# Sums of weight quarters, made once and fetched, in the second layer of an attention and two-FFN kernel

## The chip, the core and the metric
The kernel runs on one core of one Trainium2 chip. The metric is the device time of one execution in microseconds (us); a comparison uses the median of several runs. The profile is one further execution taken by the hardware profiler. The engines are named as the profile names them: PE (TensorE, matmuls; PEld its weight loads), DVE (VectorE), ACT (ScalarE), POOL (GpSimd) and SP (SyncE, which only issues transfers here).

## What is computed
Three stages follow each other, all in float32.
```
attention: 4 batches x 8 heads, 576 x 64; scores below (row maximum - tau) are masked,
           softmax, times v                                  -> x1, 2304 tokens x 512
layer 1:   sigmoid(x1 @ w_gate) * (x1 @ w_val) @ w_out       -> x2   (hidden 1536)
layer 2:   h = x2 @ w_in;  g = h if h >= 1, 0 if h <= -1, else (h + 1)^2 / 4
           g @ w_out                                         -> out  (hidden 2048)
```

## The kernel before
**Tokens and weights.** After attention the 2304 tokens are worked on in 3 passes of T = 768. Each matmul on float32 data is three: each operand is split into a rounded part that ScalarE copies and a remainder that VectorE subtracts (high by high, high by low, low by high). Activations stay in SBUF (`xall`); weights are converted once during attention and layer 1 by a chain of VectorE operations (`conversions`), written to DRAM (`saved`), and loaded again for each pass. `conversions` is a generator: a step of layer 1 takes a fixed number of items from it (`ops`), each about one VectorE operation, so that they lie beside the matmuls. Layer 1 is 36 steps (3 passes by 12 blocks of the hidden dimension): up matmuls (L480 to L482), sigmoid and product, then the down matmuls of the step before (L730).

**Layer 2** is 24 pairs of hidden blocks, 8 in each pass; pairs are numbered 0 to 23 here, so passes meet at pairs 7/8 and 15/16. The up matmul of a pair is done block-wise with seven products in place of eight, on sums of quarters. On the token side these are `x_sums`: four POOL operations a pass (L558 to L561, on 128x768), whose results and the plain quarters are split by `x_split` (L567 on ScalarE, L568 on VectorE) into seven blocks, numbered x0 to x6 and used by products 0 to 6. On the weight side they are `w_sums`: four POOL subtractions of 128x256 a pair (L576) into one tile `tsum`; `w_split` (L582, L583) splits the plain quarters and `tsum` (128x1024).

**A pair** (`pair`) issues seven products of six matmuls (L607) into two PSUM banks. Product 0's result is drained by ScalarE into `s1` (L676, the first drain); product 1's is added to it by VectorE (L665, the pair's first sum); product 3 needs the bank of that sum again. Product 2 lands on top of product 0 and is drained as `u2` (L688, the second drain); products 3 to 6 end in four more VectorE sums, of which the first is `u3` and frees the bank for product 5, and the last belongs to product 6. Then follow the activation's parts for the pair's two halves: two ScalarE squares (L615, L616), a two-input VectorE operation (L618, "STT"), the rounded half `hh` (L619) and the remainder `hl` (L621). The down matmuls (`down_pair`, 36 of them, L712) of a pair run on PE after the up matmuls of the next pair, so PE alternates: up of pair q, down of pair q - 1. `out_split` (L592, L593) splits the pair's two down weights.

**The order.** Each engine runs its own instructions in the order in which they are written. Work that lies beside matmuls is put in a list by `due(at, release, last, cost, what)` and taken out by `fill(slot, room)`: slot 3q stands behind the first drain of pair q, 3q + 1 behind its first sum, and 3q + 2 behind its last sum, that is beside the down matmuls. `fill` issues whatever has been released, by `at`, as long as `room` holds the cost, and at slot `last` in any case. All loads and stores are issued by SP, also in order: an SP instruction that waits holds the ones behind it. `finish` drains layer 1's last result (in pair 1), `store` an output pass (in pairs 9 and 17, and at the end).

Of the kernel before, what the change touches and what calls it, by code (L numbers as in the profile page):

```python
# [29 lines left out]
def kernel(  # L30
# [68 lines left out]
    }  # L99
    wides = [ps_w.tile([P, 2, 512], F32, name=f"w{i}") for i in range(3)]  # L100
# [353 lines left out]
    def ffn(att):  # L454


        with ExitStack() as st:
# [4 lines left out]
            xsp, hts = {}, {}  # L462

# [20 lines left out]
            def conversions():  # L484


                for j, (ph, f, gs) in enumerate(todo):
                    if j == 0:
                        extract(ph, gs, highs[0])
                    dst = turn() if ph == 0 else w2s[j % 2]  # L490
                    if ph == 0:
                        w32[0, 0, f] = dst
                    ops = convert(ph, gs, highs[j % 2], dst)
                    for m, _ in enumerate(ops):
                        if m == 3 + len(gs):
                            for g in todo[j + 2][2] if j + 2 < len(todo) else ():
                                load_w(todo[j + 2][0], g)
                        if m < 4 + len(gs):
                            yield
                    nc.sync.dma_start(out=saved[ph, f], in_=dst[:, : len(gs) * KD * P])  # L500
                    if j + 1 < len(todo):
                        extract(*todo[j + 1][::2], highs[(j + 1) % 2])
                    yield

# [35 lines left out]
            NQ = NF[1] // 2  # L540
            HK = KD // 2
            HC = HK * P
# [27 lines left out]
            def w_sums(q):  # L570

                w0, w1 = (w32[q][i] for i in range(2))
                b11, b21, b12, b22 = (w[:, i * HC : (i + 1) * HC] for w in (w0, w1) for i in range(2))
                t2, t3, t1, t4 = (tsum[:, i * HC : (i + 1) * HC] for i in range(4))
                for o, a, b in ((t1, b12, b11), (t2, b22, t1), (t3, b22, b12), (t4, b21, t2)):
                    nc.gpsimd.tensor_tensor(o, a, b, op=ALU.subtract)  # L576

# [11 lines left out]
            def out_split(q, i):  # L589
                src = w32[q][i][:, KD * P : 2 * KD * P]  # L590
                oh, ol = wout(q, i)
                nc.scalar.activation(oh, src, AF.Copy)  # L592
                nc.vector.tensor_tensor(ol, src, f32(oh), op=ALU.subtract)  # L593

# [50 lines left out]
            def due_x(t):  # L645
                q = t * NQ
                for i in range(7):
                    first = 3 * (q - 1) + min(i, 2)
                    last = 3 * q - 1 if i == 0 else 3 * q if i == 1 else 3 * q + 1
                    due(start(q) + i - 1, first, last, 0.93, lambda i=i: x_split(t, i))  # L650
# [7 lines left out]
            def pair(q):  # L658
# [14 lines left out]
                for i in range(2):  # L673
                    due(at - 1, 3 * q, 3 * q + 2, 0.67, lambda i=i: out_split(q, i))
                product(0, ps)
                nc.scalar.activation(s1, ps[0], AF.Copy)  # L676
                fill(3 * q, 1.9)
# [3 lines left out]
                if more:  # L681
                    w_sums(q + 1)
# [15 lines left out]
                for i in range(2):  # L698
                    g = activate(i, c[i], h[i])
                    for early, cost in ((4, 0), (3, 0.92), (1.5, 0.92)):  # L700
                        last = 3 * q + 3 if i == 0 else 3 * q + 5
                        due(at + 4 * i - early, 3 * q + 2, last, cost, lambda g=g: next(g))
                fill(3 * q + 2, LEN(q) - 7.7)
# [31 lines left out]
            def finish(t, y, slot=None):  # L735

                for i, (a, b, d) in enumerate(spans):
                    dst = xall[:, d, t * T + a - d * T : t * T + b - d * T]
                    if i % 2 == 0:
                        w = lambda dst=dst, a=a, b=b: nc.vector.tensor_copy(dst, at(y, a, b))  # L740
                    else:
                        w = lambda dst=dst, a=a, b=b: nc.scalar.activation(dst, at(y, a, b), AF.Copy)
                    if slot is None:
                        w()
                    else:
                        due(start(slot // 3) + 0.1 * i, slot, slot + 1, (1 - i % 2) * (b - a) / 800, w)

            def store(t, y, i, slot=None):
# [7 lines left out]
                def work():  # L756
                    for a in range(2) if end else (slice(None),):
                        if (i + a if end else i) % 2 == 0:
                            nc.vector.tensor_copy(o[:, a], src[:, a])
                        else:  # L760
                            nc.scalar.activation(o[:, a], src[:, a], AF.Copy)
                        nc.sync.dma_start(out=dst[:, a], in_=o[:, a])

                if slot is None:
                    work()
                else:
                    due(start(slot // 3) + 0.1 * i, slot, slot + 1, (1 - i % 2) * 0.67, work)
# [62 lines left out]
            for s in range(NS):  # L830
                nxt = order[s + 1] if s + 1 < NS else None
                ops = 8 if order[s][1] == 0 else 5
# [13 lines left out]
                elif s == NS - 2:  # L846
                    load_pair(0)
                    w_sums(0)
# [5 lines left out]
                if s == NS - 1:  # L854
# [4 lines left out]
                    fill(-1, 2.7)  # L859
# [7 lines left out]
            for q in range(NPASS * NQ):  # L867
                pair(q)
                if q == 0:
                    down(*order[-1][1:], y)  # L870
                    finish(NPASS - 1, y, 3)
                elif q < NPASS * NQ - 1:
# [3 lines left out]
                    if q % NQ == 0:  # L876
                        for i in range(T // P):
                            store(q // NQ - 1, y, i, 3 * q + 3)
# [56 lines left out]
```

## Time and profile before
| | |
|---|---|
| three runs | 1189.24, 1191.58, 1191.53 us; median 1191.53 |
| the profiled execution | 1189.46 us |
| its span, first to last instruction | 1187.6 us |
| PE, DVE, ACT, POOL busy | 95%, 72%, 52%, 23% of the span |
| mean granted clock of PE | 0.986 of full |

Matmuls are pipelined and their ends are modelled, so start times say more than busy shares. In a row of the timeline the time in brackets is how long the engine was idle before it and what ended the wait. L numbers are lines of the kernel before.

### The profile page before, as it was taken

The numbers are of one execution on the slowest core, as the hardware profiler recorded it, in microseconds if no ns is written. First come the engines' busy times: TensorE is split into PE (matmuls) and PEld (weight loads), VectorE is DVE, ScalarE is ACT, GpSimd is POOL, SyncE is SP. The second block draws the span as 40 slices with busy tenths as digits, with TensorE's granted clock in tenths as the row PEclk, the third lists the DMA queues.
The fourth block names the chain that finished last, engine by engine and source line by source line (L and its number), as shares of the span: only waits on it lengthen the run. The fifth ranks groups of instructions, "written<-read, shape, count | busy, mean of one in ns | idle before, by whom it ended". The sixth has DMA issues, their size and how long they took to land. (4 is left out here: it accounts for less than half of the span.)

```text
span 1187.6 us, 17358 instructions
## 1 busy us (share of the span) xinstructions
PE 1124.1 (95%) x6372; PEld 950.4 (80%) x6372; DVE 859.2 (72%) x1440; ACT 617.4 (52%) x1048; POOL 270.9 (23%) x423
## 2 busy tenths in 40 slices
PE   8999999999799999999999999799898998899998
PEld 5555565566799999999999999788787887778886
DVE  7888888885899988665685643676776766776663
ACT  5777777776444434433443323555455554655552
POOL 3444454453000000000000030222531234312310
PEclk9999999999899999999999999999998998999999
DMA  4323322313564665435534331122211212123101
GB/s 126 95 84 78 91 73 57 80 49 121 175 207 160 215 211 186 170 107 177 185 103 164 116 124 54 36 71 72 71 36 63 100 69 71 36 89 107 36 1 53
DMA packets 59380, 122.30 MB, mean 103 GB/s; under 512 B 8976, under 2 KB 35232, under 8 KB 59296
## 3 DMA queue, kind: packets, MB, share of 16 engines
q1 hardware_dynamic: 59152, 121.20, 31.2%
q8 instruction: 50, 0.82, 0.3%
q14 instruction: 34, 0.28, 0.1%
q10 hardware_dynamic: 144, 0.00, 0.0%
HBM read 98.57 MB, written 22.62 MB: 102 GB/s over the span
## 5 line engine op out<-in xcount | busy, mean ns | idle before, releaser
L480 PE MATMUL pgv<-xflat,win 128*128 128x384 f32 x560 | 188.5, 337 | 6.9 <-ACT act L520 4.1
L481 PE MATMUL pgv<-xflat,win 128*128 128x384 f32 x560 | 188.2, 336 | 0.0
L482 PE MATMUL pgv<-xflat,win 128*128 128x384 f32 x560 | 188.2, 336 | 0.0
L712 PE MATMUL w<-wout,hh 128*128 128x512 f32 x576 | 184.3, 394 | 0.6 <-ACT hh L619 0.6
L730 PE MATMUL w<-hh,wout 128*128 128x512 f32 (+1 forms) x576 | 147.3, 338 | 0.0
L607 PE MATMUL pu<-xflat,win 128*128 128x384 f32 x576 | 117.5, 362 | 29.2 <-DVE vals L665 28.8
L607 PEld LDWEIGHTS pu<-xflat,win 128*128 128x128 f32 x576 | 108.4, 204 | 38.2 <-DVE vals L665 33.4
L259 DVE TENSOR_SCALAR_CACHE_REDUCE s<-w,nscale 128x576 f32<-128x576 f32 x144 | 112.7, 816 | 32.8 <-PE w L250 23.0
L712 PEld LDWEIGHTS w<-wout,hh 128*128 128x128 f32 x576 | 108.1, 188 | 25.4 <-ACT hh L619 1.0
L524 DVE TENSOR_TENSOR act<-pgv,act 128x384 f32<-128x384 f32 x70 | 38.8, 554 | 118.7 <-PE pgv L482 115.1
L712 PE MATMUL w<-wout,hl 128*128 128x512 f32 x288 | 113.7, 395 | 0.5 <-DVE hl L621 0.5
L480 PEld LDWEIGHTS pgv<-xflat,win 128*128 128x128 f32 x560 | 105.7, 189 | 9.5 <-ACT act L520 4.7
L279 DVE SCALAR_TENSOR_TENSOR p<-s,mx,ex 128x576 f32<-128x576 f32 x144 | 111.9, 810 | 0.5 <-POOL lt L286 0.5
L271 ACT ACTIVATE ex<-s,mx 128x576 f32<-128x576 f32 x144 | 104.8, 775 | 6.2 <-DVE s L259 5.8
L730 PEld LDWEIGHTS w<-hh,wout 128*128 128x128 f32 x576 | 98.7, 189 | 11.4
L481 PEld LDWEIGHTS pgv<-xflat,win 128*128 128x128 f32 x560 | 105.8, 189 | 1.7 <-DVE xflat L472 0.2
L482 PEld LDWEIGHTS pgv<-xflat,win 128*128 128x128 f32 x560 | 105.8, 189 | 0.0
L520 ACT ACTIVATE act<-pgv 128x384 f32<-128x384 f32 x70 | 34.2, 489 | 135.8 <-PE pgv L482 135.7
L525 ACT ACTIVATE hh<-act 128x384 fp32r<-128x384 f32 x72 | 38.0, 527 | 121.7 <-DVE act L524 121.7
L730 PE MATMUL w<-hl,wout 128*128 128x512 f32 (+1 forms) x288 | 97.5, 338 | 0.0
L293 PEld LDWEIGHTS w<-ident,p 128*128 128x128 f32 x576 | 62.8, 141 | 41.6 <-ACT ex L271 36.6
L558 POOL TENSOR_TENSOR ssum<-xall 128x768 f32<-128x768 f32 x3 | 7.1, 2354 | 377.3 <-DVE high L163 377.3
(134 smaller groups left out, 2129.2 us busy)
## 6 DMA issues: line engine op xcount, KB each, us to landing
wmore<-saved SPq DMA_DIRECT2D x32, 512.0 KB
words<-in_moe_w_out_dram SPq DMA_DIRECT2D x26, 512.0 KB
wmore<-saved SPq DMA_DIRECT2D x15, 768.0 KB
words<-in_moe_w_in_dram SPq DMA_DIRECT2D x16, 512.0 KB
saved<-w SPq DMA_DIRECT2D x16, 512.0 KB
w<-saved SPq DMA_DIRECT2D x16, 512.0 KB
w<-saved SPq DMA_DIRECT2D x9, 768.0 KB
words<-in_moe_w_gate_dram SPq DMA_DIRECT2D x10, 512.0 KB
```

What stands on the lines that cost most here:

```text
L259: nc.vector.tensor_scalar(t[:, e], w[:, :, :HS], nscale, None, op0=ALU.mult, op1=ALU.min, accum_out=mx[:, 0, e : e + 1])
L271: nc.scalar.activation(ex[:, e], t[:, e], AF.Exp, scale=-1.0, bias=mx[:, 0, e : e + 1])
L279: nc.vector.scalar_tensor_tensor(pr[:, e], t[:, e].rearrange("p a b -> p (a b)"), mx[:, 1, e : e + 1], ex[:, e].rearrange("p a b -> p (a b ...
L293: nc.tensor.transpose(wt[:, e, cs], pr[:, e, cs], ident)
L480: nc.tensor.matmul(ps, ih[:, i, kk], xh[:, kk, c], start=(kk == 0), stop=False)
L481: nc.tensor.matmul(ps, ih[:, i, kk], xl[:, kk, c], start=False, stop=False)
L482: nc.tensor.matmul(ps, il[:, i, kk], xh[:, kk, c], start=False, stop=(kk == KD - 1))
L524: nc.vector.tensor_tensor(act, pv, act, op=ALU.mult)
L525: nc.scalar.activation(hh[:, c], act, AF.Copy)
L607: nc.tensor.matmul(ps[bank], l[:, k], r[:, k], start=bool(new) and k == m == 0, stop=k == HK - 1 and m == 2, skip_group_check=True,)
L712: nc.tensor.matmul(y[b % 3][:, b // 3], l[:, ts_], r, start=first and m == 0, stop=last and m == 2)
L730: nc.tensor.matmul(at(y, a, b), l[:, ds_], r[:, c], start=new and m == 0, stop=last and m == 2, skip_group_check=True,)
```

## The change
It has four pieces.
1. The sums of weight quarters are made in layer 1 on VectorE, once for each of the 8 pairs of hidden blocks: `conversions` calls a new `w_sums(j)` after each second block. It writes two pieces of 128x512 into the unused third of the conversion buffers, and SP writes these to a new DRAM tensor `tsaved`. A layer-1 step of passes 1 and 2 takes six items of `conversions` instead of five.
2. In layer 2 `load_sums(q)` fetches a pair's sums (128x1024) into `tsum`, in the place of the four POOL subtractions.
3. `fill(3q)`, between the first drain and the first sum, is gone. The due times of `out_split`, `activate` and the first two x splits change with it, and the rooms of the other fills.
4. `finish` and `store` drain at once, where they stand, instead of through the list.

```diff
+    tsaved = [scratch.tile([P, 2 * KD * P], F32, name=f"tsaved_{j}") for j in range(NF[1] // 2)]
...
+                    if ph == 1 and f % 2 == 1:
+                        for _ in w_sums(f // 2):
+                            yield
+
+            def w_sums(j):
+
+                b11, b21, b12, b22 = (w[:, i * HC : (i + 1) * HC] for w in w2s for i in range(2))
+                t23, t14 = (x[:, 2 * KD * P :] for x in highs.values())
+                t2, t3, t1, t4 = (x[:, i * HC : (i + 1) * HC] for x in (t23, t14) for i in range(2))
+                for n, (o, a, b) in enumerate(((t1, b12, b11), (t2, b22, t1), (t3, b22, b12), (t4, b21, t2))):
+                    nc.vector.tensor_tensor(o, a, b, op=ALU.subtract)
+                    if n == 1:
+                        yield
+                for i, x in enumerate((t23, t14)):
+                    nc.sync.dma_start(out=tsaved[j][:, i * 2 * HC : (i + 1) * 2 * HC], in_=x)
+                yield
...
-            def w_sums(q):
-
-                w0, w1 = (w32[q][i] for i in range(2))
-                b11, b21, b12, b22 = (w[:, i * HC : (i + 1) * HC] for w in (w0, w1) for i in range(2))
-                t2, t3, t1, t4 = (tsum[:, i * HC : (i + 1) * HC] for i in range(4))
-                for o, a, b in ((t1, b12, b11), (t2, b22, t1), (t3, b22, b12), (t4, b21, t2)):
-                    nc.gpsimd.tensor_tensor(o, a, b, op=ALU.subtract)
...
+            def load_sums(q):
+                nc.sync.dma_start(out=tsum, in_=tsaved[q % NQ])
...
-                    first = 3 * (q - 1) + min(i, 2)
-                    last = 3 * q - 1 if i == 0 else 3 * q if i == 1 else 3 * q + 1
+                    first = 3 * (q - 1) + max(1, min(i, 2))
+                    last = 3 * q - 1 if i < 2 else 3 * q + 1
...
-                    due(at - 1, 3 * q, 3 * q + 2, 0.67, lambda i=i: out_split(q, i))
+                    due(at - 1.8 + 0.3 * i, 3 * q, 3 * q + 2, 0.67, lambda i=i: out_split(q, i))
                 product(0, ps)
                 nc.scalar.activation(s1, ps[0], AF.Copy)
-                fill(3 * q, 1.9)
                 product(1, ps)
                 add(c[0][:, t0], ps[1], s1)
                 fill(3 * q + 1, 1.5)
                 if more:
-                    w_sums(q + 1)
+                    load_sums(q + 1)
...
-                    for early, cost in ((4, 0), (3, 0.92), (1.5, 0.92)):
-                        last = 3 * q + 3 if i == 0 else 3 * q + 5
-                        due(at + 4 * i - early, 3 * q + 2, last, cost, lambda g=g: next(g))
-                fill(3 * q + 2, LEN(q) - 7.7)
+                    for when, cost in (((-4, 0), (-1.9, 0.92), (-1.7, 0.92)), ((-1.6, 0), (1, 0.92), (2.5, 0.92)))[i]:
+                        last = 3 * q + 2 if i == 0 else 3 * q + 5
+                        due(at + when, 3 * q + 2, last, cost, lambda g=g: next(g))
+                fill(3 * q + 2, LEN(q) - (8 if j == 0 else 6))
...
-                ops = 8 if order[s][1] == 0 else 5
+                ops = 8 if order[s][1] == 0 else 6
...
-                    w_sums(0)
+                    load_sums(0)
...
-                    fill(-1, 2.7)
+                    fill(-1, 4.4)
...
-                    finish(NPASS - 1, y, 3)
+                    finish(NPASS - 1, y)
...
-                            store(q // NQ - 1, y, i, 3 * q + 3)
+                            store(q // NQ - 1, y, i)
```

How the change moves instructions, in three places. In the names `pu` is the products' PSUM, `act` the drained `s1` and `u2`, `win` the split up weights, `wout` the split down weights, `wmore` and `w_0`, `w_1` the loaded weights, `vals`, `raw` and `rb` hidden values. Line numbers of the changed kernel differ: L688 is its first drain, L699 its second, L591 and L592 are `w_split`, L601 and L602 `out_split`, L627, L628, L630, L631, L633 the activation, L584 and L585 the x split, L575 to L578 the x sums.

ScalarE, from the first drain of pair 12 on; before:
```order
L676 ACTIVATE act<-pu 128x384
L592 ACTIVATE wout_89<-wmore 128x512
L592 ACTIVATE wout_3005<-wmore 128x512
L582 ACTIVATE win_88<-wmore 128x512
L688 ACTIVATE act<-pu 128x384
L582 ACTIVATE win_88<-tsum 128x1024
L615 ACTIVATE sqs<-vals,half 128x768
L616 ACTIVATE sqs<-sqs 128x768
L619 ACTIVATE hh<-vals 128x768
L582 ACTIVATE win_88<-wmore 128x256
L615 ACTIVATE sqs<-vals,half 128x768
L616 ACTIVATE sqs<-sqs 128x768
```
and with the change:
```order
L688 ACTIVATE act<-pu 128x384
L591 ACTIVATE win_88<-wmore 128x512
L601 ACTIVATE wout_89<-wmore 128x512
L699 ACTIVATE act<-pu 128x384
L591 ACTIVATE win_88<-tsum 128x1024
L627 ACTIVATE sqs<-vals,half 128x768
L628 ACTIVATE sqs<-sqs 128x768
L591 ACTIVATE win_88<-wmore 128x256
L631 ACTIVATE hh<-vals 128x768
L627 ACTIVATE sqs<-vals,half 128x768
L628 ACTIVATE sqs<-sqs 128x768
L601 ACTIVATE wout_3013<-wmore 128x512
```
The two out splits stood right behind the first drain, ahead of the weight split; one now stands behind the weight split, and the other one in the middle of the activation, behind the second half's squares (the last row).

VectorE, from pair 15's sums on, where the x splits of the last pass begin; before, from the first sum:
```order
L665 TENSOR_TENSOR vals<-pu,act 128x384
L583 TENSOR_TENSOR win_3004<-wmore,win_88 128x512
L593 TENSOR_TENSOR wout_6477<-wmore,wout_6477 128x512
L665 TENSOR_TENSOR high_84<-pu,act 128x384
L665 TENSOR_TENSOR vals<-pu,high_84 128x384
L665 TENSOR_TENSOR vals<-pu,act 128x384 x2
L568 TENSOR_TENSOR xmore<-xall,xmore 128x768
L583 TENSOR_TENSOR win_3004<-tsum,win_88 128x1024
L568 TENSOR_TENSOR xmore<-ssum,xmore 128x768
L568 TENSOR_TENSOR xflat<-xall,xflat 128x768
L568 TENSOR_TENSOR xflat<-ssum,xflat 128x768
L568 TENSOR_TENSOR xflat<-xall,xflat 128x768
```
and with the change, from the sums of products 4 to 6 on:
```order
L677 TENSOR_TENSOR vals<-pu,act 128x384 x2
L585 TENSOR_TENSOR xmore<-xall,xmore 128x768 x2
L592 TENSOR_TENSOR win_3012<-tsum,win_88 128x1024
L585 TENSOR_TENSOR xmore<-ssum,xmore 128x768
L585 TENSOR_TENSOR xflat<-xall,xflat 128x768
L585 TENSOR_TENSOR xflat<-ssum,xflat 128x768
L585 TENSOR_TENSOR xflat<-xall,xflat 128x768
L592 TENSOR_TENSOR win_3012<-wmore,win_88 128x256
L585 TENSOR_TENSOR xflat<-raw_86,xflat 128x768
L630 SCALAR_TENSOR_TENSOR vals<-vals,sqs 128x768
L633 TENSOR_TENSOR hl<-vals,hh 128x768
L602 TENSOR_TENSOR wout_6533<-wmore,wout_6533 128x512
```
Before, the first x split stood ahead of the first sum and the others behind the last one, mixed with the activation; now all seven stand behind the last sum and ahead of the activation, with the small weight split and one out split among them.

POOL, around the x sums of the second pass; before (L576 are weight sums):
```order
L576 TENSOR_TENSOR tsum<-wmore 128x256
L576 TENSOR_TENSOR tsum<-wmore,tsum 128x256
L576 TENSOR_TENSOR tsum<-wmore 128x256
L576 TENSOR_TENSOR tsum<-wmore,tsum 128x256
L558 TENSOR_TENSOR ssum<-xall 128x768
L559 TENSOR_TENSOR ssum<-ssum,xall 128x768
L560 TENSOR_TENSOR raw_86<-xall,ssum 128x768
L561 TENSOR_TENSOR xall<-xall 128x2x384
L576 TENSOR_TENSOR tsum<-w_1_83,w_0_82 128x256
```
and with the change, from the x sums of the first pass on:
```order
L575 TENSOR_TENSOR ssum<-xall 128x768
L576 TENSOR_TENSOR ssum<-ssum,xall 128x768
L577 TENSOR_TENSOR raw_86<-xall,ssum 128x768
L578 TENSOR_TENSOR xall<-xall 128x2x384
L575 TENSOR_TENSOR ssum<-xall 128x768
L576 TENSOR_TENSOR ssum<-ssum,xall 128x768
L577 TENSOR_TENSOR raw_86<-xall,ssum 128x768
L578 TENSOR_TENSOR xall<-xall 128x2x384
L575 TENSOR_TENSOR ssum<-xall 128x768
L576 TENSOR_TENSOR ssum<-ssum,xall 128x768
```
The x sums of the three passes follow each other on POOL with nothing between them. The first operation of each four now waits for VectorE's split x4 of the pass before, which reads the sum that it overwrites, and the third for x6.

## Rows read from the trace of the kernel before

**Rows 1.** The chain of waits, one mid-pass pair: start us, us, what
```profile
970.66 8.31 PE w L712 x36
980.43 0.63 ACT wout L592
981.70 0.68 DVE wout L593
```

**Rows 2.** Timeline, that pair: start us, us, engine, line, op, names, shapes, count [idle before]
```profile
970.70 0.56 DVE L665 TENSOR_TENSOR vals<-pu,act 128x384 f32<-128x384 f32 x1 [0.48 <-PE pu L607]
976.32 1.49 DVE L618 SCALAR_TENSOR_TENSOR vals<-vals,sqs 128x768 f32<-128x768 f32 x1
978.57 3.20 PEld L607 LDWEIGHTS pu<-xmore,win 128*128 128x128 f32 x18
978.73 0.96 DVE L621 TENSOR_TENSOR hl<-vals,hh 128x768 fp32r<-128x768 f32 x1 [0.91 <-ACT hh L619]
980.05 0.49 ACT L676 ACTIVATE act<-pu 128x384 f32<-128x384 f32 x1 [1.35 <-PE pu L607]
982.30 0.55 DVE L665 TENSOR_TENSOR vals<-pu,act 128x384 f32<-128x384 f32 x1
```

**Rows 3.** Timeline of PE, starts of product 3 in pairs 0 to 23
```profile
753.25 4.46 PE L607 MATMUL pu<-xflat,win 128*128 128x384 f32 x24 [2.08 <-DVE vals L665]
788.01 4.44 PE L607 MATMUL pu<-xflat,win 128*128 128x384 f32 x24 [0.39 <-DVE vals L665]
838.24 4.46 PE L607 MATMUL pu<-xflat,win 128*128 128x384 f32 x24 [0.81 <-DVE vals L665]
932.66 4.46 PE L607 MATMUL pu<-xflat,win 128*128 128x384 f32 x24 [0.39 <-DVE vals L665]
982.91 4.46 PE L607 MATMUL pu<-xflat,win 128*128 128x384 f32 x24 [0.81 <-DVE vals L665]
1002.15 7.11 PE L607 MATMUL pu<-xflat,win 128*128 128x384 f32 x24 [3.24 <-DVE vals L665]
1077.37 4.45 PE L607 MATMUL pu<-xflat,win 128*128 128x384 f32 x24 [0.38 <-DVE vals L665]
1161.14 4.46 PE L607 MATMUL pu<-xflat,win 128*128 128x384 f32 x24 [0.81 <-DVE vals L665]
```

**Rows 4.** L730 in one layer-1 step: window, length, PE, PEld, PEclk, DMA, GB/s
```profile
718.67:722.86 4.19, 4.19 (x24) 3.46 (x24) 1.00 0.17 65
```

**Rows 5.** One layer-1 step: window, length, busy PE PEld DVE ACT POOL, PEclk, DMA
```profile
561.00:573.50 12.50, 12.50 (x74) 11.96 (x73) 8.03 (x11) 4.52 (x8) 0.00 (x0) 1.00 0.30 92
```

**Rows 6.** Timeline of DVE, a two-input operation of 128x256
```profile
747.73 0.42 DVE L583 TENSOR_TENSOR win<-wmore,win 128x256 fp32r<-128x256 f32 x1
```

**Rows 7.** Groups of instructions by line: count, busy us, mean ns, idle before
```profile
L568 DVE TENSOR_TENSOR xmore<-xall,xmore 128x768 fp32r<-128x768 f32 x6 | 5.6, 952 | 3.3 <-ACT xmore L567 3.3
L167 DVE TENSOR_TENSOR w<-w,high 128x1024 f32<-128x1024 f32 (+2 forms) x26 | 30.7, 1181 | 0.6
L583 DVE TENSOR_TENSOR win<-tsum,win 128x1024 fp32r<-128x1024 f32 x24 | 29.2, 1216 | 0.3 <-ACT win L582 0.3
```

**Rows 8.** One us of second-layer loads, columns as in rows 5, then GB/s
```profile
931.00:932.00 1.00, 1.00 (x6) 0.95 (x6) 1.00 (x2) 1.00 (x3) 0.00 (x0) 1.00 1.02 414
```

**Rows 9.** Timeline of DVE and POOL while POOL makes x sums
```profile
853.25 3.68 DVE L593 TENSOR_TENSOR wout<-wmore,wout 128x512 fp32r<-128x512 f32 x2 [0.81 <-ACT wout L592]
856.34 2.27 POOL L561 TENSOR_TENSOR xall<-xall 128x768 f32<-128x768 f32 x1
856.85 0.55 DVE L665 TENSOR_TENSOR vals<-pu,act 128x384 f32<-128x384 f32 x1
857.32 1.84 DVE L583 TENSOR_TENSOR win<-wmore,win 128x512 fp32r<-128x512 f32 x1
```

**Rows 10.** A window across the second pass boundary, columns as in rows 5
```profile
1000.00:1020.00 20.00, 17.85 (x75) 16.30 (x76) 12.42 (x14) 7.76 (x11) 7.72 (x6) 0.83 0.17 53
```

**Rows 11.** Timeline of POOL, the longest wait of its weight sums for a load
```profile
707.62 1.11 POOL L576 TENSOR_TENSOR tsum<-wmore 128x256 f32<-128x256 f32 x1 [14.28 <-DMA wmore<-saved]
```

More of the change, by code (lines that the diff above doesn't have):

```diff
@@ L462, in ffn @@
             xsp, hts = {}, {}
+            NQ = NF[1] // 2
+            HK = KD // 2
+            HC = HK * P
             def split_xs(ph, t, a, b, ks=range(KD)):
@@ L536, in h_tiles @@
                 return tuple(hs.tile([P, T], F32R, tag=n, name=n) for n in ("hh", "hl"))
-            NQ = NF[1] // 2
-            HK = KD // 2
-            HC = HK * P
             BX = 2 * HK * HT
@@ L733, in down, with finish @@
                         )
-            def finish(t, y, slot=None):
+            def finish(t, y):
                 for i, (a, b, d) in enumerate(spans):
@@ L739, in finish, with store @@
                     if i % 2 == 0:
-                        w = lambda dst=dst, a=a, b=b: nc.vector.tensor_copy(dst, at(y, a, b))
+                        nc.vector.tensor_copy(dst, at(y, a, b))
                     else:
[L742 to L748, printed above, removed]
+                        nc.scalar.activation(dst, at(y, a, b), AF.Copy)
+            def store(t, y, i):
                 x = xall[:, :, t * T : (t + 1) * T]
@@ L754, in store @@
                 end = (t, i) == (NPASS - 1, T // P - 1)
[L756 to L767, printed above, removed]
+                for a in range(2) if end else (slice(None),):
+                    if (i + a if end else i) % 2 == 0:
+                        nc.vector.tensor_copy(o[:, a], src[:, a])
+                    else:
+                        nc.scalar.activation(o[:, a], src[:, a], AF.Copy)
+                    nc.sync.dma_start(out=dst[:, a], in_=o[:, a])
             order = [(0, t, f) for t in range(NPASS) for f in range(NF[0])]
```

## The prediction

> **What bounds the kernel now.** I read the chain of waits first, for the second layer. In a pair in mid-pass TensorE runs the 36 down matmuls, then product 0, and then the chain leaves it: ScalarE splits an out weight (L592), VectorE splits it too (L593), and only after that does VectorE add the first sum (L665) [rows 1]. So I read one pair engine by engine [rows 2]. Call the start of product 0 time 0 (978.57). The drain of product 0 (L676) starts at 1.48, 0.4 after its six matmuls were issued (6 x 0.178 = 1.07). Product 1's result is there at about 2.5 (six matmuls more), yet its add starts at 3.73, because two out splits stand ahead of it on both engines. Product 3 needs that PSUM bank. It starts at 982.91 where the 18 matmuls before it ended issuing at 981.77.
>
> Then I took the starts of product 3 over the whole layer [rows 3], to see what each stretch loses against TensorE alone. TensorE alone, a pair is 42 matmuls at 3.20 / 18 = 0.178 (7.5) and 36 down matmuls, 8.31 [rows 1, 2]: 15.83. Pair 0 is followed by the last down step of layer 1 instead, 24 matmuls in 4.19 [rows 4]: 7.5 + 4.2 = 11.7. The losses:
> - pair 0 idles 2.08; pairs 0 to 2 take 34.76 for 11.7 + 15.83: 7.2 lost; start 9.3
> - pairs 2 to 5: 50.23 for 47.49: 2.7; pairs 10 to 13: 50.25: 2.8; pairs 18 to 23: 83.77 for 79.15: 4.6. Steady 10.1, 0.92 a pair
> - pairs 5 to 10, across the first pass boundary: 94.42 for 79.15: 15.3; pairs 13 to 18, across the second: 94.46: 15.3
>
> Together 50.0 us. No edit can gain much more than that in this layer; layer 1 is TensorE without a gap (12.50 of 12.50, VectorE 8.03) [rows 5].
>
> **Part 1, weight sums in layer 1.** 8 pairs by 4 subtractions of 128x256 are added on VectorE. A two-input operation of that size took 0.42 [rows 6], so 32 x 0.42 = 13.4 us over some 19 steps, and a step now runs six conversion items instead of five, about one operation more (at most the 1.18 of the longest of these, [rows 7]). VectorE goes from 8.0 to about 10 of 12.5 in a step. TensorE covers it: cost 0. If every added us showed it would be 13.4; below 0 it can't go, since TensorE has no gap there. SP issues 16 more writes here, in program order ahead of the next step's load, which has a full step of slack; 0.
>
> **Part 2, the fetch.** SP issues 24 more loads of 512 KB, and POOL loses 96 subtractions. A load needs the old sums to have been split by VectorE, right behind the last sum of the pair before (7.9 + 0.5 + 1.2 = 9.6), and is used by ScalarE when product 5 is done, at 36 x 0.178 + 0.35 = 6.75 of the next pair: 13 us. One us of loads moved 414 KB [rows 8], so with the pair's own two loads 1.5 MB is about 4 us, estimated. Hidden; queued behind it on SP is the load of the next pair, which has a whole pair to spare. The POOL operations also held VectorE: 1.49 for an operation that took 0.96 free, twice a pair [rows 2]. Off the path before, so 0 by itself, but it gives part 3 its room.
>
> **Part 3, nothing ahead of the first sum.** With the out splits behind the sum, the add starts at 2.53 and ends at 3.08; product 2 ends issuing at 3.20, so product 3 follows without a wait (0.1 to spare). The 0.92 goes. What is late next: the out split i=1 now stands in the chain after the last sum. That chain took from 970.70 to 979.69, 8.99 [rows 2]; I take off 2 x 0.53, add the small split now ahead of it (0.82) and the out split in the middle (0.63 + 0.68, [rows 1], less overlap 0.1): 10.0. The last sum starts at 7.9 (42 x 0.178 + 0.4), so it ends at 17.9; the next first sum is due at 15.83 + 2.53 = 18.36. Room 0.45. Steady pairs: 10.1 gained, bounds 6 (half the room lost to hand-offs) and 10.1.
>
> **Part 4, the second boundary.** The seven x splits of the next pass now all run behind pair 15's last sum. On VectorE from 7.91: add 0.47, seven splits 7 x 0.87 (0.95 each [rows 7]; neighbours overlap by 0.08, as 853.25 + 3.68 against 856.85 shows [rows 9]), sum split 1.14 (1.22 less the overlap), small split 0.35, STT 0.96, then ScalarE's hh with hand-offs 0.92 [rows 2], hl 0.88, out split 0.68: 11.4, so free at 19.3, 0.95 late. The drain of pair 16, behind hh and the out split on ScalarE, starts 0.9 late, product 2 idles 0.8. Then pair 15's second square, STT and hh stand ahead of the second drain: another 1.75. Pair 16 loses 2.6, pair 17 (drains of the output first, then one half of hh ahead of the second drain) 1.0, pair 18 1.15: 4.8, with a little for the clock 5. Gain 10.3, bounds 5 (half) and 15.
>
> **Part 5, the first boundary: where POOL goes.** The x sums (L558 to L561) stood behind the weight sums in POOL's queue and so ran in pairs 6 and 14. With those gone POOL reaches them one pass early: as soon as the fifth x split, x4, has read the old sums. For pass 1 this is just before pair 0, for pass 2 in pair 7, right where VectorE has the list of part 4. What POOL does to it [rows 9]: two out splits took 3.68 (0.68 each alone, [rows 1]), and one split that started at 857.32 took 1.84, done 0.5 after POOL's operation ended at 858.61. The add at 856.85, which reads PSUM, took 0.55 as ever. So an operation with both inputs in SBUF waits for the POOL operation in flight to end, and POOL then waits for it: they alternate. A POOL operation alone is 858.61 - 856.93 = 1.7. In pair 7 the blocks fall on the small split 1.7, x6 1.7, hl 0.7, out split 1.6: 5.7 later than part 4. Drain of pair 8 starts 4.4 late (product 2 idles 4.25), its add makes product 3 idle 2.3, the second drain 1.1: 7.7. After 3.24 of idle 24 matmuls took 7.11 instead of 4.46, and the mean granted clock over 1000 to 1020 was 0.83, so between its two levels, 1.2 and 2.4 GHz [rows 3, 10]; I add 1.7. With pairs 9 and 10 (1.0 + 1.15): 11.5 where 15.3 were lost. Gain 3.8, bounds 0 and 10.
>
> The Trainium skill (SBUF — State Buffer, Who interferes with whom) says that a VectorE instruction with two SBUF inputs and a GpSimd instruction that reads SBUF exclude each other for a whole instruction, and that issue order decides who blocks. By that rule the trace agrees on the blocking (1.84 against 0.68) and on the PSUM add; but if VectorE, whose splits stand back to back, kept winning, POOL would wait, the 5.7 would vanish, and boundary 1 would come out as boundary 2: rival A.
>
> **Part 6, the start.** x3 and x4 move ahead of pair 0; x5 and x6 stay behind its first sum and each now meets a POOL operation (0.85 and 1.7): the sum u3 starts 2.7 late and product 5 idles 2.6, against 2.08 before. In pairs 1 and 2 the drains of layer 1 come first, but two out splits and hh still stand ahead of them: by the same counting 1.8 + 0.9 + 1.1, and 1.1 in pair 2: 4.9 instead of 7.2. Start 7.5, gain 1.8, bounds -1 and 6. The end (after pair 23) has the same list as before: 0.
>
> **Sum.** 10.1 + 10.3 + 3.8 + 1.8 = 26.0, less 0.5 for clock at the start: 25.5. The profiled execution took 1189.46 (span 1187.6 and 1.9 around it): 1164. The median of the runs, 1191.53, stands 2.1 above: 1166.
>
> **Rivals.**
> A. POOL's sums don't collide: VectorE wins, or POOL falls into PSUM adds. For it: POOL is short (6.8 us a pass) and PSUM adds are not held. Against: at 853 to 859 they alternated [rows 9]. Gain 6.5 more at boundary 1 and 2.6 at the start: about 35, 1157.
> B. The stall moves: the room of 0.45 in part 3 is not there, and the boundaries lose as before in another place, on ScalarE's hh ahead of the drains. For it: a chain of nine hand-offs fills all but 0.45 of a pair. Against: VectorE is freed of 1.06 a pair. Steady 6, boundary 2 5, boundary 1 0, start 0: 11 gained, 1180.
> C. The fetch is late, and that is slower. Place: ScalarE's split of the sums, behind the load, with everything of the pair queued behind it. It decides from a landing 13.5 us after issue on; each us more costs one in 23 pairs, so beyond 14.6 the 25.5 are gone, and at 15.5 us it is 46 - 25.5 = 20 slower: 1212. For it: POOL once waited 14.28 for a load [rows 11]. Against: that was two pairs' loads amid layer 1's traffic, and here 1 us moves 414 KB [rows 8].
> D. The change doesn't do what it says: another item still stands ahead of the first sum. The order shows only the drain and, at a boundary, hh behind it, so no more than 2 in 100: 1190.
>
> **Chances.** Forecast 0.58, A 0.2, B 0.15, C 0.05, D 0.02. The likeliest case alone spans 1160 to 1173 (steady 8 to 10, each boundary 3 either way). The range takes in A and nearly all of B: 1154 to 1180. Faster by over 0.2% (2.4 us, about what a measurement here can tell from no change): 0.93, within 0.2%: 0.02, slower: 0.05.
>
> **What would show it.** In the profile after: product 3 of a mid-pass pair with no wait on L665's successor and starts 15.8 to 15.9 apart (part 3). TensorE gapless in layer 1, with VectorE near 10 of 12.5 (part 1). POOL's second four x sums in the pair before the first boundary, with VectorE's splits there at 1.8 to 2.6 instead of 0.95 (part 5); the third pass's boundary without POOL and clearly shorter than the first. ScalarE never waiting for the fetched sums. It would be wrong if mid-pass pairs still stood at 16.5 or more, if the two boundaries came out alike, or if TensorE got gaps before the second layer.

## The result, and the profile after

The changed kernel takes 1163.22 us (median of 4 runs, 1162.18 to 1164.11) where the kernel before takes 1190.67: a ratio of 0.977, 95% interval 0.9753 to 0.9787. Forecast were 1166 and a range of 1154 to 1180. The profiled execution took 1163.97, its span 1161.9 against 1187.6: 25.7 less, where the sum of the prediction was 25.5. By the medians it is 27.5 less, so agreement to 0.2 is partly a matter of which executions were profiled; and that two numbers agree says little before their terms are compared. In the changed kernel the matmuls of the products are L619, the down matmuls L723, the first drain L688, the second L699, the sums L677.

The chain of waits of a pair in mid-pass (start us, us, what) answers to [rows 1]. It no longer leaves TensorE:
```profile
970.23 7.33 PE pu L619 x42
977.55 8.40 PE w L723 x36
```
The timeline of VectorE in such a pair (columns as in [rows 2]): the chain behind the last sum (977.59) ends with hl at 987.34, the next first sum starts at 988.16 and waits only for TensorE. The room is 0.82; 0.45 was forecast. One out split now stands behind that sum, the other one (983.90) in the middle of the chain:
```profile
977.59 0.56 DVE L677 TENSOR_TENSOR rb<-pu,act 128x384 f32<-128x384 f32 x1 [0.48 <-PE pu L619]
...
986.38 0.96 DVE L633 TENSOR_TENSOR hl<-rb,hh 128x768 fp32r<-128x768 f32 x1 [0.91 <-ACT hh L631]
988.16 0.56 DVE L677 TENSOR_TENSOR vals<-pu,act 128x384 f32<-128x384 f32 x1 [0.82 <-PE pu L619]
...
989.23 0.68 DVE L602 TENSOR_TENSOR wout<-w,wout 128x512 fp32r<-128x512 f32 x1
```
The timeline of PE, as [rows 3]: first the start, then starts of product 3 that bound the stretches (pairs 2, 5, 10, 13, 18, 23):
```profile
750.77 2.37 PE L619 MATMUL pu<-xflat,win 128*128 128x384 f32 x12
755.08 3.13 PE L619 MATMUL pu<-xflat,win 128*128 128x384 f32 x12 [1.94 <-DVE high L677]
...
768.96 1.40 PE L619 MATMUL pu<-xmore,win 128*128 128x384 f32 x6 [3.66 <-ACT act L688]
...
772.91 5.21 PE L619 MATMUL pu<-xflat,win 128*128 128x384 f32 x18 [0.64 <-ACT act L699]
...
790.23 4.36 PE L619 MATMUL pu<-xflat,win 128*128 128x384 f32 x24
...
837.22 4.36 PE L619 MATMUL pu<-xflat,win 128*128 128x384 f32 x24
...
887.28 1.32 PE L619 MATMUL pu<-xflat,win 128*128 128x384 f32 x6 [2.16 <-DVE vals L677]
...
890.59 6.01 PE L619 MATMUL pu<-xflat,win 128*128 128x384 f32 x18 [1.98 <-ACT act L699]
...
925.85 4.38 PE L619 MATMUL pu<-xflat,win 128*128 128x384 f32 x24
...
973.19 4.36 PE L619 MATMUL pu<-xflat,win 128*128 128x384 f32 x24
...
1056.74 3.50 PE L619 MATMUL pu<-xflat,win 128*128 128x384 f32 x19
...
1135.11 4.36 PE L619 MATMUL pu<-xflat,win 128*128 128x384 f32 x24
```
Differences of these starts, beside those of [rows 3]:

| stretch | before | after | gained | forecast |
|---|---|---|---|---|
| to product 3 of pair 0, and on to pair 2 | 753.25 + 34.76 | 750.77 + 39.46 | -2.2 | 1.8, less 0.5 for clock |
| steady: pairs 2-5, 10-13, 18-23 | 184.25 | 172.70 | 11.55 | 10.1 |
| first boundary, pairs 5-10 | 94.42 | 88.63 | 5.8 | 3.8 |
| second boundary, pairs 13-18 | 94.46 | 83.55 | 10.9 | 10.3 |
| from product 3 of pair 23 to the end | 26.46 | 26.79 | -0.3 | 0 |

The start is wrong by 3.5 and in its sign; the others gave 3.7 more than forecast.

Layer 1 in the window of [rows 5] (us; busy PE, PEld, DVE, ACT, POOL; clock) is still without a gap, VectorE at 8.64 where 8.03 stood. From 580 to 650 there is more of the sums, VectorE at 53.46 of 70 (48.83 before), and TensorE is busy for all of the 70:
```profile
561.00:573.50 12.50, 12.50 (x74) 11.96 (x73) 8.64 (x12) 4.53 (x8) 0.00 (x0) 1.00 0.39 128
```
The timeline of VectorE and POOL in pair 7 answers to [rows 9]. POOL's first sum lasts until 883.71. Since an x sum takes 1.9 where nothing holds it (third experiment), it seems to have been let in at about 881.9, when VectorE first idles (881.96); from then on each waits for the other:
```profile
878.94 0.95 DVE L585 TENSOR_TENSOR xflat<-xall,xflat 128x768 fp32r<-128x768 f32 x1
879.10 4.61 POOL L575 TENSOR_TENSOR ssum<-xall 128x768 f32<-128x768 f32 x1 [120.76 <-DVE xflat L585]
879.81 0.42 DVE L592 TENSOR_TENSOR win<-w,win 128x256 fp32r<-128x256 f32 x1
880.14 0.95 DVE L585 TENSOR_TENSOR xflat<-raw,xflat 128x768 fp32r<-128x768 f32 x1
881.01 0.95 DVE L630 SCALAR_TENSOR_TENSOR vals<-vals,sqs 128x768 f32<-128x768 f32 x1
882.88 1.66 DVE L633 TENSOR_TENSOR hl<-vals,hh 128x768 fp32r<-128x768 f32 x1 [0.91 <-ACT hh L631]
884.46 2.31 DVE L602 TENSOR_TENSOR wout<-wmore,wout 128x512 fp32r<-128x512 f32 x1
...
887.15 2.13 DVE L630 SCALAR_TENSOR_TENSOR rb<-rb,sqs 128x768 f32<-128x768 f32 x1
```
And the start, on ScalarE and VectorE. x6 takes 2.59; later the first drain of pair 1 (L688) stands behind copies of layer 1's last output (L752), which wait for VectorE's (L750), and these stand behind an out split:
```profile
751.96 2.59 DVE L585 TENSOR_TENSOR xflat<-raw,xflat 128x768 fp32r<-128x768 f32 x1
...
764.65 0.68 DVE L602 TENSOR_TENSOR wout<-wmore,wout 128x512 fp32r<-128x512 f32 x1
765.25 0.68 DVE L750 COPY xall<-w 128x512 f32<-128x512 f32 x1
765.97 1.15 ACT L752 ACTIVATE xall<-w 128x256 f32<-128x256 f32 x3 [2.31 <-DVE xall L750]
767.93 0.60 ACT L752 ACTIVATE xall<-w 128x512 f32<-128x512 f32 x1 [0.81 <-DVE xall L750]
768.42 0.48 ACT L688 ACTIVATE act<-pu 128x384 f32<-128x384 f32 x1
```

### The profile page after: what moved, and what is told of

The parts are those of the page before. It is cut to its first block, busy times and chain, and to the rows that moved or that the text cites. A ratio compares the mean times of both kernels' runs of the same rounds, so it can differ in the third digit from the quotient of the medians.

```text
span 1161.9 us, 17313 instructions
## 1 busy us (share of the span) xinstructions
PE 1118.1 (96%) x6372; PEld 949.1 (82%) x6372; DVE 848.2 (73%) x1472; ACT 619.4 (53%) x1048; POOL 166.5 (14%) x327
## 4 chain that ended last, share of the span: by engine, by line
PE 80%; DVE 11%; ACT 4%; issue 3%; DMA 1%; SPq 0%; POOL 0%; DVEq 0%; POOLq 0%; ACTq 0%
PE w L723 13%; PE pu L619 13%; PE w L741 12%; PE pgv L484 8%; PE pgv L485 8%; PE pgv L486 8%; PE av L318 6%; PE w L294 5%; PE w L251 5%; DVE s L260 2%; PE w L247 2%; DVE p L280 1%; DVE win L592 1%; DVE vals L630 1%; DVE high L164 1%
## 5 line engine op out<-in xcount | busy, mean ns | idle before, releaser
L723 PE MATMUL w<-wout,hh 128*128 128x512 f32 x576 | 184.3, 394 | 0.6 <-ACT hh L631 0.6
L723 PEld LDWEIGHTS w<-wout,hh 128*128 128x128 f32 x576 | 108.2, 188 | 25.4 <-ACT hh L631 1.1
L619 PE MATMUL pu<-xflat,win 128*128 128x384 f32 x576 | 112.8, 351 | 8.9 <-ACT act L699 4.8
L619 PEld LDWEIGHTS pu<-xflat,win 128*128 128x128 f32 x576 | 105.8, 198 | 12.5 <-ACT act L699 6.6
L723 PE MATMUL w<-wout,hl 128*128 128x512 f32 x288 | 113.7, 395 | 0.5 <-DVE hl L633 0.5
L294 PE MATMUL w<-ident,p 128*128 128x128 f32 x576 | 79.4, 278 | 13.6 <-DVE p L280 10.5
```

The source lines that it names most:

```text
L294: nc.tensor.transpose(wt[:, e, cs], pr[:, e, cs], ident)
L619: nc.tensor.matmul(ps[bank], l[:, k], r[:, k], start=bool(new) and k == m == 0, stop=k == HK - 1 and m == 2, skip_group_check=True,)
L723: nc.tensor.matmul(y[b % 3][:, b // 3], l[:, ts_], r, start=first and m == 0, stop=last and m == 2)
```

## The experiments

Ratios are to the kernel before, with 95% intervals. Each difference of PE starts named below is read as in the table.

**Order without the fetch.** POOL makes the sums again, in the new order, and layer 1 makes none:
```diff
-                    load_sums(q + 1)
+                    w_sums2(q + 1)      # four nc.gpsimd.tensor_tensor, as before
```


> The new order alone: GpSimd makes the weight sums in the second layer as before, layer 1 makes none and nothing is fetched; the order of the drains, sums, splits and copies is the new one. Theory (order): the steady pairs got shorter because nothing of the list stands ahead of the first sum. GpSimd lengthens VectorE's chain after the last sum by about 2 x 0.53 = 1.06 a pair, and the room in the profile after is 0.82 (chain ends 987.34, first sum 988.16), so mid-pass pairs stand 15.7 to 15.95 apart instead of 15.69. GpSimd's x sums are behind the weight sums again, in pairs 6 and 14, so the first boundary comes out as the second, about 5 shorter. Time 1158 to 1166. Rival (fetch): the steady gain came from taking GpSimd off VectorE's port; then mid-pass pairs go back to 16.6 to 16.8 and the time is 1180 to 1186.

1174.93, ratio 0.9868 (0.9847 to 0.9889). Pairs 2 to 5 stand 15.79, 15.77, 15.79 apart: the steady gain belongs to the order, and the rival falls. The time lies above the range for another reason. VectorE's chain now ends just as the first sum is due, and where the x sums come on top, in pairs 6 and 14, the drain is late (PE, pair 6):
```profile
853.37 1.31 PE L624 MATMUL pu<-xmore,win 128*128 128x384 f32 x6 [1.99 <-ACT act L693]
```
The second boundary takes 90.42 here and 83.55 with the fetch, the first 91.10. So 4.0 of the second's 10.9 came from the order, the rest from POOL's absence.

**The fetch without the order.** The kernel before with pieces 1 and 2:


> The fetch alone: weight sums made in layer 1 and fetched, with the old order in the second layer (list ahead of the first sum, finish and store through the list). Theory (order): product 3 still waits for the first sum behind two out splits in every mid-pass pair, 16.6 to 16.8 apart; the fetch by itself is worth 0, and GpSimd's x sums of the third pass now run one pass early, which changes the boundaries by up to 5 either way. Time 1186 to 1194. Rival (fetch): mid-pass pairs 15.7 to 15.9, time 1163 to 1175.

1185.18, ratio 0.9949 (0.9934 to 0.9964). PE in mid-pass: product 3 waits as in [rows 3], 16.82 and 16.71 apart.
```profile
823.18 4.46 PE L622 MATMUL pu<-xflat,win 128*128 128x384 f32 x24 [0.82 <-DVE vals L680]
...
839.89 4.46 PE L622 MATMUL pu<-xflat,win 128*128 128x384 f32 x24 [0.81 <-DVE vals L680]
```
The fetch by itself is worth nothing in a steady pair (16.76 on average, 16.75 before); its 0.5% lies at the boundaries (92.18 and 89.60), while the start loses: pairs 0 to 2 take 37.55 where 34.76 stood. The forecast time, 1186 to 1194, was just missed.

**x sums out of the way.** In the changed kernel, one x sum in each of pairs 2 to 5 and 10 to 13:
```diff
                 add(u3, ps[1], u2)
+                if j in (2, 3, 4, 5) and t + 1 < NPASS:
+                    ...
+                    nc.gpsimd.tensor_tensor(hold, u3[:, :1], u3[:, :1], op=ALU.add)
+                    next(late_sums[t])
```


> The changed kernel with the x sums of passes 2 and 3 held back on GpSimd: one in each of pairs 2 to 5 (and 10 to 13), behind a one-column operation that reads the third sum u3 of that pair. So GpSimd meets VectorE neither in pair 0 nor at the first boundary. Theory (collision): the 2.59 that x6 took at the start and the alternation in pair 7 go; product 5 of pair 0 no longer idles 1.94, and the first boundary (88.63 for pairs 5 to 10) falls to that of the second, 83.5. In mid-pass an x sum starts beside sums that read PSUM and costs nothing. Time 1155 to 1158. Rival 1: the first boundary's loss is not GpSimd's but belongs to the list of seven splits; 1162 to 1164. Rival 2: eight x sums in mid-pass cost what they saved (0.6 to 1.7 each, 5 to 13 in all); 1162 to 1170.

1156.54, ratio 0.9705 (0.969 to 0.9719): the theory, and both rivals fall. The first boundary takes 83.37 where it took 88.63, and the second 83.92. An x sum in mid-pass takes 1.9, and no drain in those pairs waits longer than in the changed kernel (0.44 in pairs 2 and 10, where 0.43 stood; POOL, first of eight):
```profile
789.00 0.19 POOL L703 TENSOR_TENSOR hold<-high 128x1 f32<-128x1 f32 x1 [98.85 <-DVE high L677]
789.14 1.88 POOL L576 TENSOR_TENSOR ssum<-xall 128x768 f32<-128x768 f32 x1
```
Pairs 0 to 2 fall from 39.46 to 35.39: at the start the collision costs 4.1, with 1.94 of it idle time. Most of the rest is clock, as the first of two windows of the changed kernel shows (columns as above, the clock behind POOL). The second window lies after the next idle time; there the clock is 0.51, nearly all at the lower of its two levels, 1.2 GHz:
```profile
755.00:760.00 5.00, 4.92 (x19) 4.64 (x20) 2.89 (x6) 3.03 (x4) 3.34 (x2) 0.66 0.00 0
...
770.00:775.00 5.00, 4.37 (x14) 3.86 (x13) 1.52 (x2) 2.35 (x4) 0.00 (x0) 0.51 0.00 0
```
With the x sums spread the first of these windows is at full clock; the low clock after the next idle time stays (0.54 from 765 to 770):
```profile
755.00:760.00 5.00, 5.00 (x31) 4.51 (x31) 4.05 (x6) 3.28 (x5) 0.00 (x0) 1.00 0.09 12
```
What the start still loses is mostly the first drain of pair 1, with 4.48 of idle time here and the clock behind it.

**The copies behind the first sum.** In the changed kernel:
```diff
                 add(c[0][:, t0], ps[1], s1)
+                if q == 1:
+                    finish(NPASS - 1, y)
...
-                    finish(NPASS - 1, y)
```


> The changed kernel with the copies of layer 1's last output moved behind the first sum of pair 1 (they stood ahead of pair 1's first drain). Theory (copies in the way): ScalarE's first drain of pair 1 waited for the copies that alternate between VectorE and ScalarE, and these for two out splits and hl; with the copies behind, the 3.66 and 0.64 of idle and the slow 18 matmuls (5.21 for 3.2) go: the stretch from the first drain of pair 0 to product 3 of pair 2, 41.46, becomes 35 to 37, and the time 1157 to 1159. Rival (the stall moves): the down matmuls of pair 0 need the same PSUM banks, or the second half of pair 0's activation is late next; 0 to 2 gained, 1161 to 1163.

1163.77, ratio 0.9768 (0.9753 to 0.9782): the rival, with nothing gained at all (pairs 0 to 2 take 39.61 where 39.46 stood). The first drain no longer waits; the second waits for what the first waited for, and for half an activation:
```profile
773.16 5.81 PE L619 MATMUL pu<-xflat,win 128*128 128x384 f32 x18 [5.79 <-ACT act L701]
```

**Sums and fetch doubled.** In the changed kernel:
```diff
+                    for _ in range(2):
                         nc.vector.tensor_tensor(o, a, b, op=ALU.subtract)
...
+                for _ in range(2):
                     nc.sync.dma_start(out=tsum, in_=tsaved[q % NQ])
```


> The changed kernel with every weight sum of layer 1 made twice (32 more subtractions of 128x256 on VectorE, 13.4 us more) and every fetch of the sums issued twice (24 more loads of 512 KB). Theory (both hidden): TensorE covers VectorE in layer 1, and the fetch has 13 us of window against some 4 of landing; 0 for both, 1162 to 1165, first drain of pair 0 at 748 to 749.5. Rival 1 (the sums show): every added us shows in layer 1, first drain of pair 0 up to 13 later, 1170 to 1177. Rival 2 (the fetch is on the edge): ScalarE waited 2.53 for it once, at the first boundary, so a doubled one makes later pairs wait too; 1 or more a pair, 1175 to 1190, with TensorE idle behind tsum.

1175.78, ratio 0.9874 (0.9859 to 0.9889): my theory falls, but neither rival holds as put. The first drain of pair 0 is 5.7 later than in the changed kernel (754.48 against 748.77). 1.8 of that was there before layer 1 began, where nothing differs; in layer 1, a split for the third pass made TensorE wait 1.96 (with a clock of 0.87 over 448 to 461 around it), and one operation 0.74. The rest of the added sums was covered. Steady pairs stayed (15.66, 15.74, 15.63). The remaining loss sits behind the boundaries: the first drain of pair 10 waits 3.65, that of pair 18 3.47 (PE, ScalarE and SP at pair 10):
```profile
931.15 1.31 PE L621 MATMUL pu<-xmore,win 128*128 128x384 f32 x6 [3.65 <-ACT act L690]
...
920.23 1.06 ACT L592 ACTIVATE win<-tsum 128x1024 fp32r<-128x1024 f32 x1 [6.16 <-DMA tsum<-tsaved]
...
909.30 3.17 SPq L769 DMA_DIRECT2D out_dram<-xall  x6
912.52 4.41 SPq L607 DMA_DIRECT2D tsum<-tsaved  x2
```
The fetch is issued behind six stores of the finished pass. The changed kernel has the same two places, with 2.53 and 3.33 of waiting on ScalarE, and there the waits are nearly covered: pair 10's first drain waits 0.43, pair 18's 0.81 (ScalarE, the first of the two):
```profile
913.34 1.06 ACT L591 ACTIVATE win<-tsum 128x1024 fp32r<-128x1024 f32 x1 [2.53 <-DMA tsum<-tsaved]
```

**Start once more.** With the x sums spread, copies and list items of pair 1 behind u3 (L677, third sum):
```diff
-                fill(3 * q + 1, 1.5)
+                if not (q == 1):
+                    fill(3 * q + 1, 1.5)
...
                 add(u3, ps[1], u2)
+                if q == 1:
+                    finish(NPASS - 1, y)
+                    fill(3 * q + 1, 1.5)
```


> The kernel with spread x sums, and in pair 1 both the copies of layer 1's last output and the list's items (the second half of pair 0's activation) come after the third sum u3 instead of ahead of the first and second drain. Theory (what stands ahead of the drains is the whole start loss): moving the copies alone only moved the stall from the first drain (3.66) to the second (5.79), because four copies that hand over between VectorE and ScalarE and the squares and hh stood ahead of it as well; with both behind, pair 1 runs its 42 matmuls without a gap, the first drain of pair 0 to product 3 of pair 2 goes from 37.4 (spread x sums) to 31 to 34, less 0 to 2 that pair 2 gives back: 1150 to 1154. Rival (it is the amount of work, not its place): the down matmuls of pair 0 or pair 2's first drain wait as long as pair 1 did; 1155 to 1158.

1155.61, ratio 0.9709 (0.9693 to 0.9725), against 1156.54: no difference that can be told. The theory falls; the time is the rival's, but not its place. The stall is as long as before, in front of the last product:
```profile
772.17 2.29 PE L619 MATMUL pu<-xflat,win 128*128 128x384 f32 x6 [4.97 <-DVE rb L677]
```

**Boundaries too.** The condition is `q > 0 and j < 2` instead of `q == 1` for the list:


> As the one before, and the list's items come after the third sum in the first two pairs of passes 2 and 3 too. Theory: each boundary loses some 5 (83.4 for pairs 13 to 18 against 78.8 at 15.77 a pair), of which 1.45 is the second drain of the pair behind the boundary, held by the second half of an activation, and 0.36 that of the next; these go, the waits of the first drains (0.34, 0.5, 0.4) stay or grow, 1 to 3 gained for each boundary: 2 to 6 less than the one before. Rival: the second half of the activation becomes late for the down matmuls instead, 0 to 2 slower than the one before.

1154.61, ratio 0.9696 (0.9682 to 0.9711): no difference from 1155.61 that can be told, and neither forecast. Pairs 5 to 10 take 82.83 (83.24 in the kernel before it here), 13 to 18 82.67 (83.28), where 1 to 3 each were expected: the second drain's 1.45 has become 0.47 at the last product, and pair 10's first drain, which waited 0.44, waits 1.38, behind a split of the sums that waits for the fetch:
```profile
905.58 1.06 ACT L591 ACTIVATE win<-tsum 128x1024 fp32r<-128x1024 f32 x1 [1.38 <-DMA tsum<-tsaved]
...
916.51 1.33 PE L619 MATMUL pu<-xmore,win 128*128 128x384 f32 x6 [1.38 <-ACT act L688]
```

**The fetch ahead of the stores.** In addition:
```diff
-                if more:
+                if more and q not in (NQ + 1, 2 * NQ + 1):
                     load_sums(q + 1)
...
                     if q % NQ == 0:
+                        load_sums(q + 2)
                         for i in range(T // P):
```


> As the kernel with spread x sums and the list's items behind u3 in the first two pairs of a pass, and the fetch of pairs 10's and 18's sums is issued ahead of the stores of the finished pass instead of behind them on SP's queue. Theory (the fetch is late there): behind the stores it was issued 3.2 late and ScalarE waited 2.53 for it; pair 10's and 18's first drains wait 1.38 and 1.20 in the kernel with the items behind u3, and fall to 0.4 or less; 1 to 2 gained, 1152.5 to 1153.5. Rival (the wait for the fetch is covered by slack): the drains wait as before; 1154 to 1155.5.

1153.74, ratio 0.9687 (0.9673 to 0.97). The time moved by less than the runs tell apart, but the place did what was expected: issued at 890.27, nothing waits for it, and the first drain waits 0.43:
```profile
890.27 0.32 SPq L605 DMA_DIRECT2D tsum<-tsaved  x1
...
903.26 1.04 ACT L591 ACTIVATE win<-tsum 128x1024 fp32r<-128x1024 f32 x1
...
914.74 1.31 PE L619 MATMUL pu<-xmore,win 128*128 128x384 f32 x6 [0.43 <-ACT act L688]
```
Boundaries now take 81.98 and 82.01.

**The best version.** Only the squares before the second drain of pair 1, the rest of that half behind u3, the copies behind the last sum:
```diff
+                if q == 1:
+                    fill(3 * q + 1, 0.5)
...
                 add(c[1][:, t0], ps[0], u2)
+                if q == 1:
+                    finish(NPASS - 1, y)
```


> As the one before, and in pair 1 the squares of pair 0's second half come before the second drain, the rest of that half behind u3, and the copies of layer 1's last output behind pair 1's last sum. Theory (place): nothing that waits stands ahead of a drain or a sum of pair 1, so its 42 matmuls run with at most 0.5 of idle; the copies (3.1) then hold the down matmuls of pair 0 by 1.5 to 3, against 4.95 at the last product before. First drain of pair 0 to product 3 of pair 2 falls from 38 to 34 to 36; 1150 to 1152. Rival (amount): the copies, hl and the out splits together hold the down matmuls as long as the sums were held; 1153 to 1155.

1151.68 (1151.46 to 1151.84), ratio 0.9669 (0.9656 to 0.9682): the theory, and faster than the changed kernel by another 1%. Pair 1 runs its products with 0.33 of idle time, and the copies hold the down matmuls by 2.12:
```profile
763.54 4.69 PE L619 MATMUL pu<-xflat,win 128*128 128x384 f32 x24 [0.33 <-DVE vals L677]
...
770.35 0.50 PE L733 MATMUL w<-wout,hh 128*128 128x512 f32 x1 [2.12 <-DVE xall L760]
```
Against the version before, pairs 0 to 2 take 33.17 instead of 34.84. So the place decided after all, once each item stood where TensorE had work ahead of it; moving the whole block together had only moved the stall.

## Why the prediction came out as it did

**Right: part 3, the order.** Steady pairs gained 11.55 for a forecast of 10.1. Two runs separate the causes: the order alone gives pairs of 15.79, the fetch alone 16.76. The 1.4 more is my mark for TensorE alone: I put 42 matmuls at 0.178 (7.5); they took 7.33, and pairs stand 15.70 apart instead of 15.83 (11 pairs by 0.13 is 1.4).

**Right: part 1 and, narrowly, part 2.** The sums cost layer 1 nothing: product 0 of pair 0 starts at 747.47 where 747.89 stood. VectorE rose to 8.64 of 12.5 in the window and to 9.5 of 12.5 from 580 to 650, where I had put some 10. A sum took more than the 0.42 that I had read: the group below is half of the 32, the other two groups of eight took 624 and 572, 17.9 us in all for my 13.4. And the 1.18 that I called the longest conversion is the mean of three shapes; the longest takes 1.76 (VectorE in the changed kernel, count, busy us, mean ns):
```profile
L518 DVE TENSOR_TENSOR high<-w,high 128x256 f32<-128x256 f32 x16 | 8.3, 517 | 0.3
```
The fetch cost nothing in steady pairs. But I had asked what is queued behind the fetch on SP and not what stands ahead of it: behind a boundary that is six stores. There one sign of the forecast failed, that ScalarE would never wait for the sums (2.53 and 3.33), and doubling the fetch showed how little room the stores leave.

**Right, with a cause left out: part 4.** 10.9 for 10.3. The working spoke only of the list ahead of the drains. By the run with POOL's sums that was worth 4.0; the other 6.9 came from POOL. 3.2 of it lies between the products 3 of pairs 13 and 14, where its x sums had stood, and 3.7 in the pairs behind, where it makes weight sums; that these are the cause there was not tested by itself. The loss that is left was well sized: 83.55 less five pairs of 15.70 is 5.1, for a forecast of 5.

**Right place, late beginning: part 5.** POOL reached the third pass's x sums in pair 7, as forecast, and collided with VectorE, worth 5.3 by the run that moves them away (rival A had put it at 6.5). I let the alternation begin at once, on the small split and x6. Both ran in their usual time, as did the operation behind them, and POOL's first sum lasted 4.61; only hl, the out split and the second half's STT were held, by 3.5 together where I had put 5.7. That is 1.2 of the 2.0 by which the gain of 5.8 passed 3.8; most of the rest is the 0.13 a pair again. Rival A was a part of the truth: in this pair VectorE kept winning as long as it did not pause.

**Wrong: part 6, the start, +1.3 forecast with the clock and -2.2 measured.** Two terms failed, the smaller by 1.0 and the larger by 3. The idle time of product 5 was 1.94, near my 2.6, but I added only 0.5 for the clock; the run without collision shows 4.1 for the whole. And the 4.9 for pairs 1 and 2 measured 7.9 there (35.39 less the 27.53 of TensorE alone). It counted out splits and hh ahead of the drains. The copies of layer 1's output it named ("the drains of layer 1 come first") and gave no time, although piece 4 of the change puts them straight onto both engines: they hand over from VectorE to ScalarE and back, and the first drain of pair 1 waited 3.66 behind them. They are not the whole of it: moved alone they saved nothing, and only with the rest of the block placed anew did pairs 0 to 2 take 2.2 less (33.17). How the 3 divides among the parts of the block stays open. (The two misses make 4.0, the table 3.5: product 0 had started 0.4 earlier.) That the total was close is luck: this miss and the excess of the other terms cancel.

Rival B (room not there) falls by the 0.82 measured, C by the steady pairs, D by the 25.7.

## What to carry to other kernels

Compare a forecast with its result stretch by stretch: here errors of 3.5 and 3.7 hid behind a total that was right to 0.2. An engine that is relieved of work reaches its next work earlier, and that may be the worst place: look up what stands next in its queue, and hold it back on purpose if need be. Before moving a stalling block, ask for each of its instructions what the waiting engine has left to do at the new place; in this kernel the same block cost the same in three places and less only when it was taken apart.

## What the runs showed of the hardware

Who gets through when POOL and VectorE both read SBUF was not what I expected. In pair 7 POOL's operation stood issued, by its row, from 879.10, and three VectorE operations that started after it (879.81, 880.14, 881.01) ran in their usual 0.42, 0.95 and 0.95. It took 4.61 here, and again in the kernels with late copies and with doubled sums. In the kernel with the fetch alone POOL also came 0.16 behind the start of an x split, and there the next VectorE operation had to wait:
```profile
883.49 0.95 DVE L588 TENSOR_TENSOR xflat<-xall,xflat 128x768 fp32r<-128x768 f32 x1
883.65 2.52 POOL L578 TENSOR_TENSOR ssum<-xall 128x768 f32<-128x768 f32 x1 [123.10 <-DVE xflat L588]
884.36 2.63 DVE L633 SCALAR_TENSOR_TENSOR vals<-vals,sqs 128x768 f32<-128x768 f32 x1
```
The Trainium skill (SBUF — State Buffer, Who interferes with whom) says that issue order decides who blocks. The second case agrees, 2.63 for 0.95; the first does not, and the measurement decides. What tells the two apart stays open; no run here was made for it.

Steady pairs stand 15.77 apart in the kernel with spread x sums, also in pairs 19 to 23 where POOL does nothing, against 15.68 there in the changed kernel: 24 matmuls of product 3 to 6 took 4.39 there and 4.36 here. I have no explanation; over 23 pairs it is about 2 us.
